# One ring of six tiles for keys and values, output weights in two loads, three modulation terms in one load

## The chip, the cores and the metric

The kernel runs on one core of one Trainium2 chip. The metric is the device time of one execution in microseconds (us). Before the change the median of three runs is 386.42 us (386.37 to 386.49). The profile is one execution, taken by the hardware profiler.

## The reference

One decode step of a block for 4 sequences with one token each, in float32. Six modulation terms come from the condition `c`; attention with 32 query heads over 8 key and value heads of 4096 cached tokens follows, and then a small token-mixing network.

```python
mod = (silu(c) @ w_mod).reshape(4, 6, 1, 512)        # sa, ca, ga, sb, cb, gb = terms 0 to 5
h = layernorm(x) * (1 + ca) + sa
q = h @ wq                                           # 32 heads of 128
scores = einsum("bhqd,bhkd->bhqk", q, k) * 128**-0.5 # k, v: (4, 8, 4096, 128), each used by 4 query heads
o = einsum("bhqk,bhkd->bhqd", softmax(scores), v)
x = x + ga * (o.reshape(4, 1, 4096) @ wo)
h = layernorm(x) * (1 + cb) + sb
u = gelu(einsum("bsd,sf->bdf", layernorm(h), w1) + b1)
x = x + gb * (einsum("bdf,fs->bds", u, w2) + b2).transpose(0, 2, 1)
```

Keys and values are 134 MB of the 157 MB that the core reads.

## The kernel before

The work is cut into 32 pairs, one for each sequence and key head (pair i is sequence i // 8, head i % 8). A pair needs K_i and V_i, each 128 partitions by 4096 floats, 16 KB a row. All loads are issued from SyncE's queue (SP), which works in order: a load that waits holds all that stand behind it. The sixteen DMA engines take the loads one after the other.

**Where data lies.** The pool `ring` has three slots of 32 KB a partition. A slot holds in turn the weights of terms 0 and 1 (`wm01`), half of `wq` (twice), K0 with K1 (`kk`), and then K_(i+2) with V_i (one load of 4096 KB from `kv[i]`, called kv0, kv1, ... below, issued by `load_pair`). A slot is used again when all that read it are done. Terms 2 to 4 (`wm24`) take a slot for a while, in two loads. The output weights `wo` lie outside the ring in four tiles of two heads each, called wo0, wo2, wo4 and wo6, each with a load of 2048 KB and rows of 16 KB (`load_wo`).

**The loop.** After a prologue (terms 0 and 1, the queries, the scores of pairs 0 and 1) a loop over i = 0 to 23 issues `load_pair(i + 1)`, computes the scores of pair i + 2 and their maximum, turns the exponentials of pair i + 1, projects pair i - 1 with `wo`, multiplies the weights of pair i with V_i in two halves (`values`, name `pv`), and has the exponentials of pair i + 2 taken by ScalarE in between. At the end of the pass i = 2 the terms 2 to 4 are computed (`mod`): for each a set of wide matmuls that read `wm24` (name `pm2` to `pm4`), a copy by ScalarE, a set of narrow matmuls (`pc2` to `pc4`) and another copy. After the loop the last eight pairs follow in an order written out by hand (`PLAN`), with the loads among the steps: `LP` a pair, `LK` keys, `LV` values, `LW` term 5.

The order of the loads is thus: terms 0 and 1, small inputs, wq, kk, kv0, wo0, kv1, kv2, wo2, terms 2 and 3, term 4, kv3, kv4, wo4, kv5, kv6, wo6, kv7 to kv27, K30, K31, V28 to V31, term 5.

Of the kernel before, what the change touches and what calls it, by code (L numbers as in the profile page):

```python
# [8 lines left out]
F32 = mybir.dt.float32  # L9
# [18 lines left out]
@with_exitstack  # L28
def adaln_decode(ctx: ExitStack, tc: tile.TileContext, small, x, wmod, wq, kk, kv, vv, wo, out):
    nc = tc.nc  # L30
    pad = ctx.enter_context(tc.tile_pool(name="pad", bufs=1))
    ring = ctx.enter_context(tc.tile_pool(name="ring", bufs=3))
    wos = ctx.enter_context(tc.tile_pool(name="wos", bufs=1))
# [13 lines left out]
    xr = wk.tile([P, D], F32, name="xr", tag="yw", bufs=1)[0:B]  # L47
    wm01 = ring.tile([P, 2, 4, D], F32, name="wm01", tag="kv")
    nc.sync.dma_start(wm01, wmod[0])
    nc.sync.dma_start(sm, small)  # L50
    nc.sync.dma_start(xr, x)
    wqt = []
    for k in range(0, 4, 2):
        t = ring.tile([P, 2, HQ * DH], F32, name=f"wq{k}", tag="kv")
        nc.sync.dma_start(t, wq[k // 2])
        wqt += [t[:, 0], t[:, 1]]
    w1, b1, w2 = sm[:, 0:NF], sm[:, NF:2 * NF], sm[:, 2 * NF:3 * NF]
# [98 lines left out]

    KT, VT, WM = {}, {}, {}

    def slots():
        return ring.tile([P, 2, SK], F32, name="kv", tag="kv")  # L160

    def key(t, i):
        KT[i] = t

    def value(t, i):
        VT[i] = t.rearrange("p (j d) -> p j d", d=DH)

    def load_first():
        t = slots()
        nc.sync.dma_start(t, kk)  # L170
        key(t[:, 0], 0)
        key(t[:, 1], 1)

    def load_pair(i):
        t = slots()
        nc.sync.dma_start(t, kv[i])
        key(t[:, 0], i + 2)
        value(t[:, 1], i)

    def load_wo(h):  # L180
        nc.sync.dma_start(wo_p[h // 2], wo[h // 2])

    def load_wm24():
        w = ring.tile([P, 3, 4, D], F32, name="wm24", tag="kv")
        nc.sync.dma_start(w[:, 0:2], wmod[1])
        nc.sync.dma_start(w[:, 2], wmod[2][:, 0])
        for e in range(3):
            WM[2 + e] = w[:, e]

    def load_wm5():  # L190
        t = slots().rearrange("p s (k n) -> p (s k) n", n=D)
        nc.sync.dma_start(t[:, 0:4], wmod[2][:, 1])
        WM[5] = t[:, 0:4]
        return t[:, 4:6]

    def load_key(t, i):
        nc.sync.dma_start(t, kv[i - 2][:, 0])
        key(t, i)

    def load_v(t, i, cuts):  # L200
        value(t, i)
        src = (kv[i][:, 1] if i < NS - 2 else vv[i - NS + 2]).rearrange("p (j d) -> p j d", d=DH)
        for lo, hi in zip(cuts, cuts[1:]):
            nc.sync.dma_start(VT[i][:, lo:hi], src[:, lo:hi])

# [20 lines left out]
    def scores(i):  # L226
        b, h = divmod(i, HKV)
        S[i] = s = ps_s.tile([P, 1024], F32, name=f"s{i}", tag="s")
        for n in range(2):
            for c in range(4):  # L230
                mm(s[32 * c:32 * c + 32, n * 512:(n + 1) * 512], QT[:, b, h, :],  # L231
                   KT[i][:, (n * 4 + c) * 512:(n * 4 + c + 1) * 512], start=True, stop=True)

    def row_max(i):
# [50 lines left out]
    def values(i, ks):  # L285
        if ks[0] == 0:
            PV[i] = ps_v.tile([P, 4 * DH], F32, name="pv", tag="pv")
        pT = PL[i][0]
        for k in ks:
            q = k % 4  # L290
            mm(PV[i][32 * q:32 * q + 32, :], pT[:, 128 * k:128 * k + 128:4],  # L291
               VT[i][:, 4 * k:4 * k + 4, :].rearrange("p j d -> p (j d)"), start=(k < 4), stop=(k >= 4))

    def values_narrow(i, ks, pv=None):
        if ks[0] == 0:
            PV[i] = ps_v.tile([P, DH], F32, name="pvn", tag="pv") if pv is None else pv
        pv = PV[i]
        pT = PL[i][0].rearrange("p (k r) -> p k r", r=32)
        top = 32 if i < NS - 1 else 30
        for k in ks:  # L300
            for j in range(4 * k, min(4 * k + 4, top)):
                c = j % 4
                mm(pv[32 * c:32 * c + 32, :], pT[:, j, :], VT[i][:, j, :], start=(k == 0), stop=(j + 4 >= top))  # L303

    def values_turned(i):
# [31 lines left out]
    def project(i, pa=None, between=None):  # L337
        b, h = divmod(i, HKV)
        oT = OT[i]
        if pa is None:  # L340
            pa = ps_m.tile([P, D], F32, name="pa", tag="m")
            for g in range(REP):
                mm(pa[32 * g:32 * g + 32, :], oT[:, g:g + 1].to_broadcast([P, 32]), wo_t[h][:, g, :],  # L343
                   start=True, stop=True)
        else:
            for g in range(REP):
                for c in range(4):
                    mm(pa[32 * c:32 * c + 32, :], oT[:, g:g + 1].to_broadcast([P, 32]),  # L348
                       wo_t[h][:, g, c * P:(c + 1) * P], start=(g == 0 and h == HKV - 2),
                       stop=(g == REP - 1 and h == HKV - 1))  # L350
                if between and g == 1:
                    between()
# [199 lines left out]
    def finish(b, pg, py, hb, wr):  # L552
        uu = ring.tile([P, 16, D], F32, name="uu", tag="kv")
        for js in ((0,), (1,), (2, 3, 4), (5, 6, 7), (8, 9, 10), (11, 12), (13,)):
# [34 lines left out]
    def fold_gate(gate, es):  # L589
        for e in es:  # L590
            w = wo_t[HKV - 2 + e // REP][:, e % REP]
            dv.tensor_tensor_reduce(w, w, gate, 1.0, 0.0, OP.mult, OP.add, rowsum[:, e:e + 1])
# [15 lines left out]

    load_first()
    load_pair(0)  # L610
    load_wo(0)
    for i in range(2):
# [5 lines left out]
    for i in range(NS - HKV):  # L618
        load_pair(i + 1)
        if i in (1, 3, 5):  # L620
            load_wo(i + 1)
        if i == 1:
            load_wm24()
        scores(i + 2)
# [22 lines left out]
        if mix:  # L647
            mix.outer(i % HKV)
        if i == 2:
            for t in range(2, 5):  # L650
# [4 lines left out]
                else:  # L655
                    nc.scalar.activation(dst, pm, AF.Copy)
        if i == NS - HKV - 2:
            gate = spread_gate()
# [3 lines left out]
    mix, row = Mixer(B - 2), Mixer(B - 1)  # L662
    pve = pgx = pc = ep = spare = slot = None
    gates = list(range(2 * REP))
    cuts = {NS - 1: (0, 16, 24, 28, 30, 32), NS - 2: (0, 16, 32)}
    last, halves = [(0, 1, 2, 3), (4, 5), (6,), (7,)], [(0, 1), (2, 3), (4, 5), (6, 7)]
    PLAN = """
    a23 v24.0 A23 p23 t25.0 P23 F R v24.1 LP25 G s26 t25.1 M H V24 LP26 Q a24 S26 v25.0 N s27 x A24 f p24 g
    x LP27 m26 S27 P24 m27 X26 X27 b26 B26 e26 x b27 v25.1 c g t26.1 l25 t26.0 B27 s28 V25 c g L25
    v26.0 v26.1 S28 x l26 f a25 L26 V26 A25 x m28 p25 LT X28 e27 c a26 P25 t27.0 A26 b28 s29 f B28 p26 e28  # L670
    LK30 t27.1 S29 P26 v27.0 m29 l27 g LK31 T t28.1 X29 LT t28.0 s30 L27 S30 b29 v27.1 B29 e29 l28 m30 V27
    LV28 L28 a27 g X30 t29.1 t29.0 l29 L29 s31 A27 LV29 b30 p27 x B30 S31 c c m31 e30 P27 X31 v28.0 f LT LV30
    b31 v28.1 B31 f e31 LV31 l30 V28 L30 t30.1 l31 L31 a28 t31.1 A28 p28 v29.0 v29.1 t30.0 f P28 V29 v30.0 a29
    v30.1 A29 LW p29 f v30.2 v30.3 t31.0 P29 g V30 Y y a30 A30 p30 E x v31.0 f v31.1 v31.2 v31.3 V31 z31 a31 I A31 j p31
    g T2 zs za zx zq c c zm zb0 T3 zv zb1 zw0 zn zc
    """
# [7 lines left out]
    for step in PLAN.split():  # L684
# [17 lines left out]
        elif op == "p":  # L702
            project(i, pgx[:, 4] if i >= NS - 2 else None, mean_last if i == NS - 1 else None)
        elif op == "LT":
            slot = slots()
        elif op == "LK":
            load_key(slot[:, i % 2], i)
        elif op == "LV":
            load_v(slot[:, i % 2], i, cuts.get(i, (0, 32)))
        elif op == "LW":  # L710
            spare = load_wm5()
        elif op == "x":
            mix.expand(spare if mix.n == 6 else None)
        elif op == "f":
# [74 lines left out]
```

## Time and profile before

| | |
|---|---|
| median of three runs | 386.42 us |
| span of the profiled execution, first to last instruction | 384.7 us |
| TensorE matmul busy | 298.7 us (78%) |
| VectorE busy | 198.2 us (52%) |
| ScalarE busy | 112.2 us (29%) |
| read from HBM | 157.32 MB |
| mean granted TensorE clock | 0.883 |

The profiled execution's span leaves out what lies around the first and the last instruction; no time of its own besides the span is given, so it is read against the runs, which are 1.7 us longer. Rows of a timeline have the start, the length, the engine, the line of the kernel, the operation, what is written and read, a count, and in brackets the idle time before and what ended it. L231 is the scores, L291 the values, L215 and L221 the wide and narrow matmuls of the terms 2 to 4. SPq is SyncE's queue, L176 a pair's load, L181 a load of `wo`, L170 the load `kk`, L49 that of terms 0 and 1. Rows of waits have the waiting engine and line, the one waited for, the total in us, the times and the longest. Rows of stretches give for each engine its busy time, then the granted clock of TensorE (PEclk), the busy share of the DMA engines and GB/s.

### The profile page before, as it was taken

What the parts mean: (1) busy time and instruction counts of PE and PEld (TensorE: products, weight loads), DVE (VectorE), ACT (ScalarE), POOL (GpSimd) and SP (SyncE); (2) the same over time, 40 slices, a digit from 0 to 9 for tenths busy, and PEclk for the clock granted to TensorE, in tenths of its full rate; (3) what the DMA queues carried; (4) which work ended last, traced back from release to release, by engine and by line L of the source; (5) the groups of instructions that cost most, each with busy time, mean ns of one, the idle gap of its engine ahead of it and who ended that gap; (6) DMA issues with size and microseconds to landing.
All of it is one profiled execution on the core that took longest, in us unless ns stands there. A gap on an engine that the chain in (4) does not pass through costs nothing.

```text
span 384.7 us, 5604 instructions
## 1 busy us (share of the span) xinstructions
PE 298.7 (78%) x2380; PEld 117.2 (30%) x2380; DVE 198.2 (52%) x407; ACT 112.2 (29%) x144; POOL 7.7 (2%) x33
## 2 busy tenths in 40 slices
PE   0856777866966949979877878788888887999984
PEld 0112122311323313334322222342222343333653
DVE  1130251620451424664866545557665567778757
ACT  1001111121110110212567311124575105657276
POOL 1100000000000000000000000000000000000000
PEclk9989555985695685998999998999999999999999
DMA  8999999999999999999999999999999999999930
GB/s 331 433 433 436 411 453 433 409 432 436 423 441 433 434 436 436 434 436 431 429 425 433 428 433 434 429 433 431 429 434 436 434 436 432 424 417 423 418 122 3
DMA packets 7409, 157.69 MB, mean 410 GB/s; under 512 B 964, under 2 KB 1236, under 8 KB 1496
## 3 DMA queue, kind: packets, MB, share of 16 engines
q1 hardware_dynamic: 7376, 157.33, 95.4%
q8 instruction: 18, 0.29, 0.3%
q14 instruction: 7, 0.06, 0.0%
q10 hardware_dynamic: 8, 0.00, 0.0%
HBM read 157.32 MB, written 0.01 MB: 409 GB/s over the span
## 4 chain that ended last, share of the span: by engine, by line
DMA 60%; PE 29%; DVE 7%; ACT 2%; issue 1%; POOL 0%; SPq 0%; POOLq 0%; DVEq 0%
DMA kv<-in_kv 58%; PE s L231 8%; PE pv L291 7%; PE s L122 2%; PE qs L138 2%; DVE m L236 2%; DVE p L267 2%; DMA sm<-in_small 2%; PE pa L343 2%; PE pt L328 2%; ACT uu L562 1%; PE pb L251 1%; PE pve L303 1%; PE pm L240 1%; PE pgx L348 1%
## 5 line engine op out<-in xcount | busy, mean ns | idle before, releaser
L231 PE MATMUL s<-kv,QT 128*32 128x512 f32 x512 | 75.2, 714 | 38.9 <-DMA kv<-in_kv 37.0
L236 DVE TENSOR_REDUCE m<-s 128x1 f32<-128x1024 f32 x32 | 39.2, 1224 | 96.0 <-PE s L231 95.9
L261 ACT ACTIVATE p<-s,nm 128x1024 f32<-128x1024 f32 x32 | 35.7, 1115 | 180.6 <-DVE nm L256 180.5
L291 PE MATMUL pv<-kv,p 128*32 128x512 f32 x464 | 69.8, 670 | 0.7 <-DMA kv<-in_kv 0.7
L231 PEld LDWEIGHTS s<-kv,QT 128*32 128x32 f32 x512 | 15.8, 123 | 84.0 <-DMA kv<-in_kv 52.5
L328 PEld LDWEIGHTS pt<-g,po 128*128 128x128 f32 x236 | 31.1, 205 | 27.2 <-issue 19.9
L343 PE MATMUL pa<-wo,oT 128*32 128x512 f32 x240 | 34.6, 648 | 4.6 <-DVE oT L335 4.4
L328 PE MATMUL pt<-g,po 128*128 128x4 f32 (+2 forms) x236 | 33.9, 267 | 1.5 <-DVE po L314 1.0
L267 DVE STREAM_TRANSPOSE p<-p 128x1024 f32<-128x1024 f32 x25 | 30.9, 1234 | 0.0
L314 DVE COPY po<-pv 128x512 f32<-128x512 f32 x29 | 20.0, 688 | 16.8 <-PE pv L291 16.7
L245 DVE TENSOR_REDUCE mx<-pm 1x128 f32<-1x512 f32 x32 | 21.3, 669 | 1.1 <-PE pm L240 1.1
L442 DVE TENSOR_SCALAR u<-hb,wr,sm 128x512 f32<-128x512 f32 x40 | 19.9, 541 | 1.9 <-POOL wr L437 1.0
L506 ACT ACTIVATE u<-u 128x1024 f32<-128x1024 f32 x20 | 20.4, 1051 | 1.5 <-DVE u L442 1.4
L361 DVE TENSOR_TENSOR acc<-acc,pa 128x512 f32<-128x512 f32 x26 | 17.8, 686 | 4.3 <-PE pa L343 4.2
L261 ACT ACT_TABLE_LOAD x11 | 14.1, 1283 | 20.3 <-DVE nm L256 20.2
L251 PEld LDWEIGHTS pb<-neg,mx 1*128 1x128 f32 x64 | 10.4, 202 | 28.2 <-DVE mx L245 26.5
L122 PE MATMUL s<-wm,sT 128*4 128x512 f32 x16 | 9.1, 732 | 10.6 <-DVE sT L108 10.6
L506 ACT ACT_TABLE_LOAD x13 | 16.7, 1283 | 0.2
L291 PEld LDWEIGHTS pv<-kv,p 128*32 128x32 f32 x464 | 13.4, 146 | 7.2 <-issue 3.1
L240 PE MATMUL pm<-ident,m 128*1 128x128 f32 x32 | 9.3, 289 | 7.4 <-DVE m L236 3.5
L251 PE MATMUL pb<-neg,mx 1*128 1x1 f32 x64 | 13.1, 271 | 2.1 <-DVE mx L245 2.1
L453 PE MATMUL py<-u,sm 128*32 128x512 f32 x80 | 14.4, 616 | 0.0
(158 smaller groups left out, 214.7 us busy)
## 6 DMA issues: line engine op xcount, KB each, us to landing
kv<-in_kv SPq DMA_DIRECT2D x28, 4096.0 KB, 21.9
wq<-in_wq SPq DMA_DIRECT2D x2, 4096.0 KB, 16.3
wo<-in_wo SPq DMA_DIRECT2D x4, 2048.0 KB
kv<-in_kv SPq DMA_DIRECT2D x4, 2048.0 KB, 20.3
wm<-in_wmod SPq DMA_DIRECT2D x2, 2048.0 KB, 14.8
kv<-in_kk SPq DMA_DIRECT2D x1, 4096.0 KB
kv<-in_vv SPq DMA_DIRECT2D x3, 1024.0 KB
wm<-in_wmod SPq DMA_DIRECT2D x1, 1024.0 KB
```

What stands on the lines that cost most here:

```text
L231: mm(s[32 * c:32 * c + 32, n * 512:(n + 1) * 512], QT[:, b, h, :], KT[i][:, (n * 4 + c) * 512:(n * 4 + c + 1) * 512], start=True, stop=True)
L236: dv.tensor_reduce(M[i], S[i], axis=AX.X, op=OP.max)
L245: dv.tensor_reduce(mx, M[i].rearrange("o (c r) -> o r c", c=4).unsqueeze(1).to_broadcast([1, 4, 32, 4]), axis=AX.X, op=OP.max)
L251: mm(pb, M[i].rearrange("o c r -> o (c r)"), neg1, start=True, stop=True)
L261: nc.scalar.activation(p, S[i], AF.Exp, bias=M.pop(i), accum_out=l)
L267: dv.transpose(PL[i][0], PL[i][0])
L291: mm(PV[i][32 * q:32 * q + 32, :], pT[:, 128 * k:128 * k + 128:4], VT[i][:, 4 * k:4 * k + 4, :].rearrange("p j d -> p (j d)"), start=(k < ...
L314: dv.tensor_copy(PV[i], pv)
L328: mm(pt, po[:, c * DH:(c + 1) * DH], sel.unsqueeze(1).to_broadcast([P, m, REP]), start=(c == 0), stop=(c == n - 1))
L343: mm(pa[32 * g:32 * g + 32, :], oT[:, g:g + 1].to_broadcast([P, 32]), wo_t[h][:, g, :], start=True, stop=True)
L442: dv.tensor_scalar(u[:, e, :], hb, wr[:, j:j + 1], b1[:, j:j + 1], op0=OP.mult, op1=OP.add)
L506: nc.scalar.activation(u, u, AF.Gelu_apprx_tanh)
```

## The change

The three slots become one tile `RING` of six parts of 16 KB a partition, of which a pair's load takes two neighbours. The four tiles of `wo` become one, `wo_t`, loaded in two loads of 4096 KB with rows of 32 KB (heads 0 to 3, heads 4 to 7: wo0-3 and wo4-7 below). Terms 0 and 1 are loaded into the place of heads 0 and 1 of `wo_t`, terms 2 to 4 with one load of 3072 KB and rows of 24 KB into the place of heads 4 to 6. A list `LOADS` has all later loads in order; `advance(name)` is called when the code that reads a part has been written, and issues from the head of the list what may go: a pair when what its two parts held has been read, wo0-3 after terms 0 and 1, wo4-7 after terms 2 to 4 (`"M2"`). The terms 2 to 4 are computed at the end of the pass i = 1 instead of i = 2. The steps for loads are gone from `PLAN`.

```diff
-    wm01 = ring.tile([P, 2, 4, D], F32, name="wm01", tag="kv")
-    nc.sync.dma_start(wm01, wmod[0])
+    RING = ring.tile([P, 6, SK], F32, name="kv")
+    wo_t = wos.tile([P, HKV, REP, D], F32, name="wo")
+    wm01, wm24 = wo_t[:, 0:2], wo_t[:, 4:7]
+    nc.sync.dma_start(wm01, wm0)
...
-    wo_p = [wos.tile([P, 2, REP, D], F32, name=f"wo{h}") for h in range(0, HKV, 2)]
-    wo_t = [wo_p[h // 2][:, h % 2] for h in range(HKV)]
...
+    held, read = [("Q", 0), ("Q", 0), ("Q", 1), ("Q", 1), None, None], {None, ("Q", 0), ("Q", 1)}
...
+    def queue():
+        q = [entry(["K0", "K1"], kk)]
+        for i in range(NS - 4):
+            q.append(entry([f"K{i + 2}", f"V{i}"], kv[i]))
+        for i in (NS - 2, NS - 1):
+            q.append(entry([f"K{i}"], kv[i - 2][:, 0]))
+        for i in range(NS - 4, NS):
+            q.append(entry([f"V{i}"], kv[i][:, 1] if i < NS - 2 else vv[i - NS + 2]))
+        q.append(entry(["W5"], wm5))
+        q.insert(2, ("wo", "M0", wo_t[:, 0:4], wo[0]))
+        q.insert(4, ("wo", None, wm24, wm2))
+        q.insert(6, ("wo", "M2", wo_t[:, 4:8], wo[1]))
+        return q
+
+    LOADS, at = queue(), [4]
+
+    def advance(name=None):
+        read.add(name)
+        while LOADS:
+            kind, names, *rest = LOADS[0]
+            if kind == "wo":
+                if names not in read:
+                    return
+                nc.sync.dma_start(*rest)
+            else:
+                n, p = len(names), at[0]
+                if any(h not in read for h in held[p:p + n]):
+                    return
...
+                held[p:p + n] = names
+                at[0] = (p + n) % 6
...
+            LOADS.pop(0)
...
-        load_pair(i + 1)
-        if i in (1, 3, 5):
-            load_wo(i + 1)
-        if i == 1:
-            load_wm24()
...
-        if i == 2:
+        if i == 1:
             for t in range(2, 5):
                 pm = mod(t)
...
+            advance("M2")
```

What it does to SyncE's queue, from the load of wq on. `DMAHW` stands for a counter of landed loads (there are eight, taken in turn), `PE` for a wait on TensorE. Before, the terms 2 to 4 (`wm_337`) come after kv2 and wo2, and their slot is asked for by kv5, the row after wo4 (`wo_130`):

```order
L176 DMA kv<-in_kv 128x8192 [waits DMAHW3_49,PE_49]
L181 DMA wo_128<-in_wo 128x4096
L176 DMA kv<-in_kv 128x8192 [waits DMAHW4_49,PE_49]
L176 DMA kv<-in_kv 128x8192 [waits DMAHW5_49,DMAHW1_49,PE_49]
L181 DMA wo_129<-in_wo 128x4096 [waits DMAHW2_49]
L185 DMA wm_337<-in_wmod 128x4096 [waits DMAHW6_49,PE_49]
L186 DMA wm_337<-in_wmod 128x2048
L176 DMA kv<-in_kv 128x8192 [waits DMAHW0_49,PE_49]
L176 DMA kv<-in_kv 128x8192 [waits DMAHW1_49,PE_49]
L181 DMA wo_130<-in_wo 128x4096 [waits DMAHW7_49]
L176 DMA kv<-in_kv 128x8192 [waits DMAHW4_49,DMAHW3_49,PE_49]
```

After, from kk on: the terms (`in_wm`, 128x6144) stand between kv1 and kv2, and the load after kv2 is wo4-7:

```order
L204 DMA kv<-in_kk 128x8192
L204 DMA kv<-in_kv 128x8192 [waits DMAHW3_49,PE_49]
L186 DMA wo<-in_wo 128x8192 [waits DMAHW0_49]
L204 DMA kv<-in_kv 128x8192 [waits DMAHW4_49,PE_49]
L186 DMA wo<-in_wm 128x6144 [waits DMAHW1_49]
L204 DMA kv<-in_kv 128x8192 [waits DMAHW5_49,DMAHW2_49,PE_49]
L186 DMA wo<-in_wo 128x8192 [waits DMAHW1_49,PE_49]
L204 DMA kv<-in_kv 128x8192 [waits DMAHW6_49]
L204 DMA kv<-in_kv 128x8192 [waits DMAHW0_49]
L204 DMA kv<-in_kv 128x8192 [waits DMAHW2_49,PE_49]
```

So the load that waits for the reading of the terms has moved from three loads behind them to one load behind them, and kv3 and kv4, which ask for no later reading, have moved behind it.

On TensorE, the end of the pass i = 2 before (the values of pair 2, the three terms, the scores of pair 5, `s5`):

```order
L291 MATMUL pv_427<-kv_334,p_325 32x512 x4
L251 MATMUL pb_432<-neg1_87,mx_425 128x1
L291 MATMUL pv_427<-kv_334,p_325 32x512 x4
L215 MATMUL pm2_445<-wm24_337,sT8_134 32x512 x4
L221 MATMUL pc2_452<-ym_450,g32_122 32x128 x4
L215 MATMUL pm3_458<-wm24_337,sT8_134 32x512 x4
L221 MATMUL pc3_465<-ym_463,g32_122 32x128 x4
L215 MATMUL pm4_471<-wm24_337,sT8_134 32x512 x4
L221 MATMUL pc4_478<-ym_476,g32_122 32x128 x4
L231 MATMUL s5_487<-kv_392,QT_124 32x512 x8
```

And the end of the pass i = 1 after it (the values of pair 1, the terms read from `wo`, the scores of pair 4, `s4`):

```order
L300 MATMUL pv_362<-kv_90,p_282 32x512 x4
L260 MATMUL pb_367<-neg1_87,mx_360 128x1
L300 MATMUL pv_362<-kv_90,p_282 32x512 x4
L223 MATMUL pm2_380<-wo_91,sT8_129 32x512 x4
L229 MATMUL pc2_387<-ym_385,g32_121 32x128 x4
L223 MATMUL pm3_393<-wo_91,sT8_129 32x512 x4
L229 MATMUL pc3_400<-ym_398,g32_121 32x128 x4
L223 MATMUL pm4_406<-wo_91,sT8_129 32x512 x4
L229 MATMUL pc4_413<-ym_411,g32_121 32x128 x4
L239 MATMUL s4_422<-kv_90,QT_123 32x512 x8
```

The three terms have moved ahead of the scores of pair 4, one pass earlier; the rest of TensorE's order is the same.

More of the change, by code (lines that the diff above doesn't have):

```diff
@@ L28, in adaln_decode @@
 @with_exitstack
-def adaln_decode(ctx: ExitStack, tc: tile.TileContext, small, x, wmod, wq, kk, kv, vv, wo, out):
+def adaln_decode(ctx: ExitStack, tc: tile.TileContext, small, x, wm0, wm2, wm5, wq, kk, kv, vv, wo, out):
     nc = tc.nc
     pad = ctx.enter_context(tc.tile_pool(name="pad", bufs=1))
-    ring = ctx.enter_context(tc.tile_pool(name="ring", bufs=3))
+    ring = ctx.enter_context(tc.tile_pool(name="ring", bufs=1))
     wos = ctx.enter_context(tc.tile_pool(name="wos", bufs=1))
@@ L53, in adaln_decode @@
     for k in range(0, 4, 2):
-        t = ring.tile([P, 2, HQ * DH], F32, name=f"wq{k}", tag="kv")
-        nc.sync.dma_start(t, wq[k // 2])
-        wqt += [t[:, 0], t[:, 1]]
+        nc.sync.dma_start(RING[:, k:k + 2], wq[k // 2])
+        wqt += [RING[:, k], RING[:, k + 1]]
     w1, b1, w2 = sm[:, 0:NF], sm[:, NF:2 * NF], sm[:, 2 * NF:3 * NF]
@@ L155, in adaln_decode @@
     nc.scalar.activation(prep[:, 0], px, AF.Copy)
[L157 to L204, printed above, removed]
+    KT, VT, WM = {}, {}, {2 + e: wm24[:, e] for e in range(3)}
+    held, read = [("Q", 0), ("Q", 0), ("Q", 1), ("Q", 1), None, None], {None, ("Q", 0), ("Q", 1)}
@@ new lines, in adaln_decode, with entry @@
+    cuts = {NS - 1: (0, 16, 24, 28, 30, 32), NS - 2: (0, 16, 32)}
+    def entry(names, src):
+        return ("ring", names, src)
+    def queue():
[11 more added lines that the diff above has]
+        return q
@@ new lines, in adaln_decode @@
+    LOADS, at = queue(), [4]
[11 more added lines that the diff above has]
+                    return
+                for k, nm in enumerate(names):
+                    t, i = RING[:, p + k], int(nm[1:])
+                    if nm[0] == "K":
+                        KT[i] = t
+                    elif nm[0] == "V":
+                        VT[i] = t.rearrange("p (j d) -> p j d", d=DH)
+                    else:
+                        WM[i] = t.rearrange("p (k n) -> p k n", n=D)[:, 0:4]
+                held[p:p + n] = names
+                at[0] = (p + n) % 6
+                if names[0] == "W5":
+                    nc.sync.dma_start(WM[5], rest[0])
+                elif len(names) > 1:
+                    nc.sync.dma_start(RING[:, p:p + n], rest[0])
+                elif names[0][0] == "K":
+                    nc.sync.dma_start(RING[:, p], rest[0])
+                else:
+                    cs = cuts.get(i, (0, 32))
+                    v = rest[0].rearrange("p (j d) -> p j d", d=DH)
+                    for lo, hi in zip(cs, cs[1:]):
+                        nc.sync.dma_start(VT[i][:, lo:hi], v[:, lo:hi])
+            LOADS.pop(0)
@@ L232, in scores @@
                    KT[i][:, (n * 4 + c) * 512:(n * 4 + c + 1) * 512], start=True, stop=True)
+        advance(f"K{i}")
     def row_max(i):
@@ L292, in values @@
                VT[i][:, 4 * k:4 * k + 4, :].rearrange("p j d -> p (j d)"), start=(k < 4), stop=(k >= 4))
+        if ks[-1] == 7:
+            advance(f"V{i}")
     def values_narrow(i, ks, pv=None):
@@ L303, in values_narrow @@
                 mm(pv[32 * c:32 * c + 32, :], pT[:, j, :], VT[i][:, j, :], start=(k == 0), stop=(j + 4 >= top))
+        if ks[-1] == 7:
+            advance(f"V{i}")
     def values_turned(i):
@@ L342, in project @@
             for g in range(REP):
-                mm(pa[32 * g:32 * g + 32, :], oT[:, g:g + 1].to_broadcast([P, 32]), wo_t[h][:, g, :],
+                mm(pa[32 * g:32 * g + 32, :], oT[:, g:g + 1].to_broadcast([P, 32]), wo_t[:, h, g, :],
                    start=True, stop=True)
@@ L348, in project @@
                     mm(pa[32 * c:32 * c + 32, :], oT[:, g:g + 1].to_broadcast([P, 32]),
-                       wo_t[h][:, g, c * P:(c + 1) * P], start=(g == 0 and h == HKV - 2),
+                       wo_t[:, h, g, c * P:(c + 1) * P], start=(g == 0 and h == HKV - 2),
                        stop=(g == REP - 1 and h == HKV - 1))
@@ L552, in finish @@
     def finish(b, pg, py, hb, wr):
-        uu = ring.tile([P, 16, D], F32, name="uu", tag="kv")
+        uu = RING[:, 4:6].rearrange("p s (k n) -> p (s k) n", n=D)
         for js in ((0,), (1,), (2, 3, 4), (5, 6, 7), (8, 9, 10), (11, 12), (13,)):
@@ L590, in fold_gate @@
         for e in es:
-            w = wo_t[HKV - 2 + e // REP][:, e % REP]
+            w = wo_t[:, HKV - 2 + e // REP, e % REP]
             dv.tensor_tensor_reduce(w, w, gate, 1.0, 0.0, OP.mult, OP.add, rowsum[:, e:e + 1])
@@ L607, in mean_last @@
         dv.tensor_copy(mu, pm)
-    load_first()
-    load_pair(0)
-    load_wo(0)
+    advance("M0")
     for i in range(2):
@@ L662, in adaln_decode @@
     mix, row = Mixer(B - 2), Mixer(B - 1)
-    pve = pgx = pc = ep = spare = slot = None
+    pve = pgx = pc = ep = None
     gates = list(range(2 * REP))
-    cuts = {NS - 1: (0, 16, 24, 28, 30, 32), NS - 2: (0, 16, 32)}
     last, halves = [(0, 1, 2, 3), (4, 5), (6,), (7,)], [(0, 1), (2, 3), (4, 5), (6, 7)]
     PLAN = """
[L668 to L674, printed above, removed]
+    a23 v24.0 A23 p23 t25.0 P23 F R v24.1 G s26 t25.1 M H V24 Q a24 S26 v25.0 N s27 x A24 f p24 g
+    x m26 S27 P24 m27 X26 X27 b26 B26 e26 x b27 v25.1 c g t26.1 l25 t26.0 B27 s28 V25 c g L25
+    v26.0 v26.1 S28 x l26 f a25 L26 V26 A25 x m28 p25 X28 e27 c a26 P25 t27.0 A26 b28 s29 f B28 p26 e28
+    t27.1 S29 P26 v27.0 m29 l27 g T t28.1 X29 t28.0 s30 L27 S30 b29 v27.1 B29 e29 l28 m30 V27
+    L28 a27 g X30 t29.1 t29.0 l29 L29 s31 A27 b30 p27 x B30 S31 c c m31 e30 P27 X31 v28.0 f
+    b31 v28.1 B31 f e31 l30 V28 L30 t30.1 l31 L31 a28 t31.1 A28 p28 v29.0 v29.1 t30.0 f P28 V29 v30.0 a29
+    v30.1 A29 p29 f v30.2 v30.3 t31.0 P29 g V30 Y y a30 A30 p30 E x v31.0 f v31.1 v31.2 v31.3 V31 z31 a31 I A31 j p31
     g T2 zs za zx zq c c zm zb0 T3 zv zb1 zw0 zn zc
@@ L703, in adaln_decode @@
             project(i, pgx[:, 4] if i >= NS - 2 else None, mean_last if i == NS - 1 else None)
[L704 to L711, printed above, removed]
         elif op == "x":
-            mix.expand(spare if mix.n == 6 else None)
+            mix.expand(RING[:, 2].rearrange("p (k n) -> p k n", n=D)[:, 4:6] if mix.n == 6 else None)
         elif op == "f":
@@ L770 @@
     v = a["A_v_cache"].reshape(NS, P, SK * DH // P)
+    wm = a["w_mod"].reshape(4, P, 6, D).transpose(1, 2, 0, 3)
     arrays = {
@@ L773 @@
         "x": con(a["A_x"].reshape(B, D)),
-        "wmod": con(a["w_mod"].reshape(4, P, 3, 2, D).transpose(2, 1, 3, 0, 4)),
+        "wm0": con(wm[:, 0:2]),
+        "wm2": con(wm[:, 2:5]),
+        "wm5": con(wm[:, 5]),
         "wq": con(a["A_wq"].reshape(2, 2, P, HQ * DH).transpose(0, 2, 1, 3)),
@@ L778 @@
         "vv": con(v[NS - 2:]),
-        "wo": con(a["A_wo"].reshape(HKV // 2, 2, REP, DH, D).transpose(0, 3, 1, 2, 4)),
+        "wo": con(a["A_wo"].reshape(2, 4, REP, DH, D).transpose(0, 3, 1, 2, 4)),
     }
```

3 lines of the change are left out of this document (1 added, 2 removed).

## The prediction

> **What bounds the kernel now.** I read the page's slices first, then the chain, then the stretches of time, and last the load queue beside TensorE around the place of the change.
>
> ```profile
> span 384.7 us, 5604 instructions
> ...
> DMA  8999999999999999999999999999999999999930
> GB/s 331 433 433 436 411 453 433 409 432 436 423 441 433 434 436 436 434 436 431 429 425 433 428 433 434 429 433 431 429 434 436 434 436 432 424 417 423 418 122 3
> DMA packets 7409, 157.69 MB, mean 410 GB/s; under 512 B 964, under 2 KB 1236, under 8 KB 1496
> ...
> DMA 60%; PE 29%; DVE 7%; ACT 2%; issue 1%; POOL 0%; SPq 0%; POOLq 0%; DVEq 0%
> ```
> ```profile
> core 0: us, PE busy (x) PEld busy (x) DVE busy (x) ACT busy (x) POOL busy (x), PEclk, DMA share, GB/s
> 2.00:3.00 1.00, 0.00 (x0) 0.00 (x0) 0.94 (x2) 0.00 (x1) 0.00 (x0) 1.00 0.39 82
> 3.00:83.00 80.00, 53.34 (x291) 15.79 (x291) 23.34 (x47) 7.93 (x17) 2.31 (x15) 0.81 1.00 431
> 3.00:366.00 363.00, 286.33 (x2116) 108.93 (x2120) 184.67 (x370) 98.13 (x126) 6.27 (x24) 0.88 1.00 431
> ```
> The DMA engines are busy from 3 us to 366 us without a pause (share 1.00 at 431 GB/s), and TensorE keeps up. So the kernel is one stream of 157 MB and what is left to compute when its last keys come. The reader should take two things from this: a change that moves no fewer bytes can gain only in the rate, and any time in which the queue runs empty is paid in full, since nothing later can catch up. The end hangs on the stream as well:
>
> ```profile
> 343.17 1.92 PE L231 MATMUL s<-kv,QT 128*32 128x512 f32 x16 [0.60 <-DMA kv<-in_kv]
> ```
> TensorE waits there for the keys of a late pair, and from there on the chain is compute in an order that the change leaves alone. The work after it comes later by what the keys come later.
>
> **The change, part by part.** The runs are at 386.42 us and this execution spans 384.7, so 1.7 us lie around the span. I sum against 384.7 and add 1.7.
>
> *Kept in place, in a new order.* The bytes are the same, but what stands in the queue at the start is not. Before, the queue has wo0 (2048 KB), kv1, kv2, wo2, the two loads of terms 2 to 4, kv3. After, it has wo0-3 (4096 KB), kv1, terms 2 to 4 (3072 KB), kv2, wo4-7, kv3. The load of wo4-7 writes over the three terms, so it has to wait until TensorE has read the last of them, and SyncE issues in order, so kv3 and all that follows wait behind it. In the trace the wait on the terms costs nothing, because a lot is in flight. The sizes (count, KB each) from the page's load issues, the wait as SyncE's queue had it, and SyncE's issues in time:
>
> ```profile
> kv<-in_kv SPq DMA_DIRECT2D x28, 4096.0 KB, 21.9
> wq<-in_wq SPq DMA_DIRECT2D x2, 4096.0 KB, 16.3
> wo<-in_wo SPq DMA_DIRECT2D x4, 2048.0 KB
> ...
> wm<-in_wmod SPq DMA_DIRECT2D x2, 2048.0 KB, 14.8
> kv<-in_kk SPq DMA_DIRECT2D x1, 4096.0 KB
> ...
> wm<-in_wmod SPq DMA_DIRECT2D x1, 1024.0 KB
> ```
> ```profile
> SPq L176 <- PE pm L215: 6.5, 1, 6.5
> ```
> ```profile
> 0.72 0.39 SPq L49 DMA_DIRECT2D wm<-in_wmod  x1
> ...
> 19.72 0.33 SPq L170 DMA_DIRECT2D kv<-in_kk  x1
> ...
> 71.80 8.61 SPq L176 DMA_DIRECT2D kv<-in_kv  x2
> 80.45 0.42 SPq L181 DMA_DIRECT2D wo<-in_wo  x1
> 91.49 14.30 SPq L176 DMA_DIRECT2D kv<-in_kv  x2
> ```
> Row 71.80 holds kv3 and kv4. kv5 waits for the terms and is issued at 91.49, when they are read. Issued by then are kv3, kv4 and wo4 on top of all before, 45.1 MB; at 431 GB/s and 34.6 MB by 83 us that lasts to about 107 us, so 16 us of cover. After the change the load that waits stands right behind kv2. [...]
>
> *When the queue runs empty.* Up to the end of kv2 the new order has 2048 + 38 KB (terms 0, 1 and the small inputs), 8192 (wq), five loads of 4096 (kk, kv0, wo0-3, kv1, kv2) and 3072 KB: 34.64 MB. The rows above give 0.08 + 80 x 0.431 = 34.56 MB by 83.0 us. So it ends at 83.2 us.
>
> *When the terms are read.* TensorE in the stretch that matters:
>
> ```profile
> 59.52 1.08 PE L291 MATMUL pv<-kv,p 128*32 128x512 f32 x4
> 63.14 3.30 PE L231 MATMUL s<-kv,QT 128*32 128x512 f32 x16 [2.54 <-DMA kv<-in_kv]
> ...
> 70.64 1.09 PE L291 MATMUL pv<-kv,p 128*32 128x512 f32 x8
> ```
> ```profile
> 82.51 1.47 PE L215 MATMUL pm<-wm,sT 128*32 128x512 f32 x8 [2.49 <-DMA wm<-in_wmod]
> 84.67 0.66 PE L221 MATMUL pc<-ym,g 128*32 128x128 f32 x8 [0.70 <-ACT ym L218]
> 85.73 1.94 PE L215 MATMUL pm<-wm,sT 128*32 128x512 f32 x8 [0.40 <-ACT prep L656]
> 88.44 0.66 PE L221 MATMUL pc<-ym,g 128*32 128x128 f32 x8 [0.78 <-ACT ym L218]
> 89.49 1.94 PE L215 MATMUL pm<-wm,sT 128*32 128x512 f32 x8 [0.40 <-ACT prep L656]
> ```
> ```profile
> 94.58 3.64 PE L231 MATMUL s<-kv,QT 128*32 128x512 f32 x16 [1.72 <-DMA kv<-in_kv]
> ```
> ```profile
> 63.10:71.80 8.70, 8.22 (x53) 2.74 (x53) 3.92 (x7) 0.80 (x1) 0.00 (x0) 0.83 0.97 420
> 94.50:105.40 10.90, 10.82 (x57) 4.07 (x61) 4.04 (x7) 0.79 (x1) 0.00 (x0) 0.59 0.97 418
> 118.80:131.00 12.20, 12.14 (x57) 4.33 (x61) 4.04 (x7) 1.21 (x2) 0.00 (x0) 0.51 0.98 422
> 143.20:155.20 12.00, 11.95 (x57) 4.33 (x61) 4.04 (x7) 1.21 (x2) 0.00 (x0) 0.52 1.01 437
> 82.50:91.50 9.00, 6.65 (x40) 0.97 (x40) 0.00 (x0) 1.75 (x4) 0.00 (x0) 0.53 1.06 455
> ```
> The last fence is a table of stretches, with the columns named above. (1) kv1 is in at 63.1 before. With 2048 KB more ahead of it, 2.10 MB / 0.431 = 4.9 us, scores of pair 3 start at 68.0. (2) Then the rest of that pass of the loop runs, to the second half of values(1). The row of 63.10 shows 8.6 us for it, at a mean clock of 0.83; three other passes that start after TensorE had stood still took 10.9, 12.2 and 12.0 us, at clocks near one half. After the change TensorE stands still before it from 60.6 to 68.0, longer than before, so it starts cold like those. I take the mean of the four, 10.9. The terms' load is in by then: it follows kv1 by 3.15 MB / 0.431 = 7.3 us, so at 75.3 us. (3) The three terms: before, 8.9 us from the first matmul to the last reading (82.51 to 91.43), nearly all at half clock (0.53). At full clock the two kinds of matmul take about half of 1.94 and 0.66 us, and the waits for ScalarE (0.78 and 0.40) stay: 2 x (0.97 + 0.78 + 0.33 + 0.40) + 0.97 = 5.9 us, an estimate. After a cold pass the clock has just come back, but three short terms with pauses hardly hold it; I take 7.2, in the middle. Together: 68.0 + 10.9 + 7.2 = 86.1 us. At the ends: 68.0 + 8.6 + 5.9 = 82.5, and 68.0 + 12.2 + 8.9 = 89.1.
>
> *The restart.* wo4-7 starts into an empty queue. The nearest row is the start of the program: the first load is issued at 0.72 us, and the stream has its full rate from 3.0 with 82 GB/s in the microsecond before, so the stream runs as if it had begun somewhat after 2; some engines move data before that. I bound it by 1.0 and 1.9 us and take 1.5. [...] No row shows a restart in mid-kernel.
>
> So the stream stands still from 83.2 to 86.1 + 1.5 = 87.6: 4.4 us. At the ends: 82.5 + 1.0 - 83.2 = 0.3, and 89.1 + 1.9 - 83.2 = 7.8 us. Nothing hides it: wo4-7, kv3 and kv4 then go out together (29 us of stream), and kv5 asks only for values(2), which ends some 12 us after the terms, so the queue fills again.
>
> *Longer rows and fewer loads.* wo goes from four loads of 16 KB rows to two of 32 KB, terms 2 to 4 from 16 and 8 KB rows to 24 KB: 11.5 MB.
>
> ```profile
> 4.00:7.00 3.00, 0.00 (x0) 0.00 (x0) 0.00 (x0) 0.00 (x0) 0.00 (x0) 1.00 1.02 437
> 10.00:26.00 16.00, 11.20 (x28) 2.39 (x32) 4.93 (x17) 0.00 (x0) 1.28 (x5) 0.97 1.01 436
> 355.00:361.00 6.00, 5.54 (x106) 4.10 (x102) 4.36 (x11) 3.02 (x4) 0.00 (x0) 1.00 1.00 425
> ```
> The three rows move 16 KB rows, 32 KB rows and mostly 8 KB rows. Between 437 and 436 there is no gain; between 425 and 436, 11.5 MB take 0.7 us less. I take 0.2, nearer to the row with 16 KB, which most of it had.
>
> *The ring of six.* Keys are let go after the scores, values after their own matmuls, each for itself; pairs still ask for both. Before 63 us and in the last 60 us the queue is never empty (share 1.00), so earlier issues only lengthen the queue: 0. kk no longer waits for the first terms: it was issued at 19.72, when terms 0 and 1 and wq, 10.5 MB, still had the queue until about 27 us; 0. Were that cover gone, each such load would start up to 1.9 us late, as the restart. The three terms move ahead of one pass on TensorE, ScalarE and VectorE: the scores of pair 4 start after them, some 3 us after kv2 is in, and the exponentials of pair 4 behind ScalarE's copies; the wait for pair 5, whose keys come at about 108 us, covers both, else it would be those 3 us. Address changes on TensorE and the `uu` tile that lies in two ring tiles: 0, the same instructions on the same engines.
>
> Sum: 384.7 + 4.4 - 0.2 = 388.9, and 1.7 around it: 390.6 us.
>
> **Rivals.** (B) *The clock comes back early.* If full clock is granted within the first scores, as at 63.10 (8.6 us), the terms are read at about 68.0 + 8.6 + 6.6 = 83.2 and the stop is 1.5 us: 384.7 + 1.5 - 0.2 + 1.7 = 387.7. For it: that very pass did so before. Against: three of the four rows with a cold start did not. [...]
>
> (C) *The stop is hidden.* If the terms are read before 81.7 (83.2 less the restart), nothing is left of it: 386.2. It needs less than the lowest sum of (2) and (3), 14.5, by nearly a microsecond.
>
> (D) *Faster.* Fewer, longer loads raise the rate: 0.7 us as above at most, and for each of the three loads saved the difference between 436 GB/s here and 431 in the long run, 4.19 MB / 0.431 - 4.19 MB / 0.436 = 0.1 us, 0.3 in all: 385.4. It decides only if the stop is under 1 us, that is if the terms are read by about 82.7. For it: the earliest sum, 82.5. [...]
>
> (E) *More than the one stop.* TensorE stays at half clock and needs 12 us for a pass while a pair's data needs 9.7, so kv6 to kv9 are issued late and the queue runs out again; some 3 us more: 394. Against it: the row at 94.50 recovers within its pass.
>
> **Chances.** A (forecast) 0.58, B 0.24, C 0.07, D 0.04, E 0.07. A's own range is 388.7 to 393; with most of B below and the bound of 7.8 us above (394.0, rarely reached) the range is 387.2 to 393.6. A measurement of this kernel can tell about 0.2%, 0.8 us. Faster by that is D, 0.04; within it are C and the lowest edge of B, 0.08; slower the rest, 0.88.
>
> **What would show it.** The GB/s of the slice around 83 to 88 us should fall (by up to half of a 9.6 us slice), and the DMA share be 1.00 before and after. The issue of wo4-7 should wait for TensorE's last reading of the terms, at 84 to 89 us, with kv3 and kv4 right behind it. Scores of pair 3 should start near 68, those of pair 5, which stand behind wo4-7 and kv3, near 108 instead of 94.6, and from the pass after wo6 of before on everything should lie about 4 us later. The keys awaited at 343.1 should come near 347. I am wrong if the queue never runs empty, if TensorE reads the terms before 82, or if the late keys come at the same time in spite of a stop.

## The result and the profile after

The change makes the kernel slower by 0.7%: 388.51 us median of 11 executions against 386.49, a ratio of 1.0072 (95% interval 1.005 to 1.0093). The 11 times lie in two groups: seven from 387.78 to 388.57 us, at a mean granted clock of 0.898 to 0.915, and four from 391.47 to 391.91 us, at 0.873 to 0.886. The profiled execution took 388.26 us and spans 386.5, 1.8 us more than the one before. By its time it belongs to the lower group, so its trace should show the smaller stop of the two.

The page of the changed kernel, the slices of 9.66 us:

```profile
span 386.5 us, 5592 instructions
...
PEclk9989666799589699899999998969999989899999
DMA  8999999989999999999999999999999999999920
GB/s 330 434 434 434 432 434 418 450 348 432 434 432 434 429 427 434 432 434 432 434 433 431 430 434 432 434 434 432 434 432 434 432 434 430 421 424 422 416 106 4
```

One slice falls out of the row, the ninth (77 to 87 us) with 348 GB/s. Before, no slice between the first and the tail is under 409. SyncE's queue and TensorE there, in the changed kernel:

```profile
47.20 0.33 SPq L204 DMA_DIRECT2D kv<-in_kv  x1
82.81 0.33 SPq L186 DMA_DIRECT2D wo<-in_wo  x1
83.19 236.24 SPq L204 DMA_DIRECT2D kv<-in_kv  x25
```
```profile
67.60 3.64 PE L239 MATMUL s<-kv,QT 128*32 128x512 f32 x16 [9.14 <-DMA kv<-in_kv]
71.17 1.33 PE L341 MATMUL pt<-g,po 128*128 128x4 f32 x8
...
76.43 1.04 PE L223 MATMUL pm<-wo,sT 128*32 128x512 f32 x8
78.19 0.43 PE L229 MATMUL pc<-ym,g 128*32 128x128 f32 x8 [0.72 <-ACT ym L226]
79.02 1.06 PE L223 MATMUL pm<-wo,sT 128*32 128x512 f32 x8 [0.40 <-ACT prep L662]
80.86 0.43 PE L229 MATMUL pc<-ym,g 128*32 128x128 f32 x8 [0.78 <-ACT ym L226]
81.68 1.06 PE L223 MATMUL pm<-wo,sT 128*32 128x512 f32 x8 [0.40 <-ACT prep L662]
...
105.27 3.64 PE L239 MATMUL s<-kv,QT 128*32 128x512 f32 x16 [13.43 <-DMA kv<-in_kv]
```

From 47.2 us on SyncE issues nothing until TensorE has read the last term (81.68 + 1.06 = 82.74): wo4-7 goes out at 82.81, kv3 behind it. The first scores are at half clock (3.64 us), and the next matmuls are already quicker (1.33 us where a cold pass before had 1.87): the granted clock is 0.50 up to 71.5 us and 1.00 from 72 to 95. The stretches around it (columns: busy time of PE, PEld, DVE, ACT, POOL, then PEclk, DMA share, GB/s):

```profile
75.00:82.00 7.00, 4.71 (x50) 1.39 (x50) 1.01 (x3) 2.96 (x6) 0.00 (x0) 1.00 1.04 447
82.00:84.50 2.50, 1.17 (x16) 0.16 (x8) 0.29 (x1) 0.60 (x1) 0.00 (x0) 1.00 0.80 236
90.00:366.00 276.00, 222.07 (x1755) 89.12 (x1747) 160.60 (x319) 89.06 (x106) 3.96 (x9) 0.93 1.00 431
```

The queue ran empty between 82 and 84.5 us, and never again. (A packet of data counts in the stretch in which it starts, so that a share can be a little over 1.) The delay shows far behind. The scores of pair 17, which wait for their keys, before and after:

```profile
220.80 1.93 PE L231 MATMUL s<-kv,QT 128*32 128x512 f32 x16 [0.51 <-DMA kv<-in_kv]
```
```profile
222.29 1.92 PE L239 MATMUL s<-kv,QT 128*32 128x512 f32 x16 [0.36 <-DMA kv<-in_kv]
```

They come 1.5 us later. The theory is thus: the whole cost is the time in which the stream stops, and it is set by the moment at which TensorE has read the terms; two groups of times are there because the clock of TensorE sets that moment. The rivals: the cost lies in the layout (ring of six, one tile of output weights, rows); or part of a stop is taken up by slack later; or the groups have another cause than the clock.

### The profile page after: what moved, and what is told of

Same layout as the page of the kernel before. It is cut to its first block, busy times and chain, and to the rows that moved or that the text cites. A ratio compares the mean times of both kernels' runs of the same rounds, so it can differ in the third digit from the quotient of the medians.

```text
span 386.5 us, 5592 instructions
## 1 busy us (share of the span) xinstructions
PE 289.3 (75%) x2380; PEld 114.1 (30%) x2380; DVE 198.0 (51%) x407; ACT 112.2 (29%) x144; POOL 7.7 (2%) x33
## 4 chain that ended last, share of the span: by engine, by line
DMA 55%; PE 31%; DVE 10%; ACT 2%; issue 1%; SPq 1%; POOL 0%; POOLq 0%
DMA kv<-in_kv 46%; DMA kv<-in_kk 9%; PE s L239 9%; PE pv L300 8%; DVE m L245 3%; PE pa L356 3%; DVE p L276 3%; PE pt L341 2%; PE pb L260 1%; PE py L466 1%; ACT kv L575 1%; PE pve L314 1%; PE pm L249 1%; DVE po L327 1%; PE pl L284 1%
## 5 line engine op out<-in xcount | busy, mean ns | idle before, releaser
L239 PE MATMUL s<-kv,QT 128*32 128x512 f32 x512 | 72.5, 690 | 53.2 <-DMA kv<-in_kv 50.8
L300 PE MATMUL pv<-kv,p 128*32 128x512 f32 x464 | 68.2, 656 | 0.0
L239 PEld LDWEIGHTS s<-kv,QT 128*32 128x32 f32 x512 | 14.6, 117 | 95.6 <-DMA kv<-in_kv 68.8
L260 PEld LDWEIGHTS pb<-neg,mx 1*128 1x128 f32 x64 | 9.6, 187 | 27.1 <-DVE mx L254 25.4
L121 PE MATMUL s<-wo,sT 128*4 128x512 f32 x16 | 8.7, 702 | 10.4 <-DVE sT L107 10.4
L260 PE MATMUL pb<-neg,mx 1*128 1x1 f32 x64 | 12.3, 259 | 2.1 <-DVE mx L254 2.1
```

Source lines behind the costliest of these rows:

```text
L260: mm(pb, M[i].rearrange("o c r -> o (c r)"), neg1, start=True, stop=True)
```

## The experiments

**A pair between.** The list is changed by one place, so that kv3 goes ahead of the load that waits.

```diff
-        q.insert(6, ("wo", "M2", wo_t[:, 4:8], wo[1]))
+        q.insert(7, ("wo", "M2", wo_t[:, 4:8], wo[1]))
```

> The changed kernel with one entry of the list moved: kv3 goes ahead of wo4-7, so the load that waits for the terms has 4.19 MB (9.7 us) more in flight. If the whole cost is the stop of the queue, the stop is gone at either clock (terms read by 89 us at the latest, the stream lasts to 93), all executions lie together and the time is 386.2 to 386.6, the kernel before within 0.2%; the share of the DMA engines is 1.00 from 80 to 95 us. If the cost lies in the ring of six, the one tile of output weights or the row lengths, it stays at 388 and 391.5 us.

Measured: 386.55 us (386.49 to 386.61 in 11 executions), ratio to the kernel before 0.9998 (0.9989 to 1.0007). Its issues and its keys of pair 17:

```profile
47.42 11.01 SPq L204 DMA_DIRECT2D kv<-in_kv  x2
83.05 0.33 SPq L186 DMA_DIRECT2D wo<-in_wo  x1
```
```profile
220.72 1.92 PE L239 MATMUL s<-kv,QT 128*32 128x512 f32 x16 [0.43 <-DMA kv<-in_kv]
```

wo4-7 waits as long as in the changed kernel, to 83.05, but kv3 is in flight meanwhile. The cost is gone, and with it the two groups, though the mean clock still varies from 0.887 to 0.925. So the layout, the ring of six and the longer rows together cost nothing and gain nothing that the runs can tell: all of the loss hangs on that one place in the list.

**The terms a pass earlier.** The other way out: wo4-7 stays behind kv2, but the terms are loaded ahead of kv1 and computed at the end of the pass i = 0.

```diff
-        q.insert(4, ("wo", None, wm24, wm2))
+        q.insert(3, ("wo", None, wm24, wm2))
...
-        if i == 1:
+        if i == 0:
             for t in range(2, 5):
```

> The changed kernel with the load of the terms 2 to 4 one place earlier, ahead of kv1, and the terms computed at the end of the pass i = 0, where TensorE waits for kv1 anyway. wo4-7 still stands right behind kv2 and still waits for the terms. The terms land at about 66 us and are read by 72 at full and 75 at half clock, some 8 us before the queue would run empty at 83. If only the moment at which the waiting load is released counts, the stop is gone in all executions: 386.3 to 386.7, as where a pair was put between. If a load that waits right behind kv2 costs something in itself, or if kv1 coming 7 us later does (its pass then ends later), the time is 387.5 or more.

Measured: 386.56 us (386.40 to 386.66 in 12 executions), ratio 0.9997 (0.9988 to 1.0006).

```profile
65.35 1.94 PE L223 MATMUL pm<-wo,sT 128*32 128x512 f32 x8 [8.42 <-DMA wo<-in_wm]
...
72.82 1.94 PE L223 MATMUL pm<-wo,sT 128*32 128x512 f32 x8 [0.40 <-ACT prep L662]
...
75.96 3.64 PE L239 MATMUL s<-kv,QT 128*32 128x512 f32 x16
```
```profile
74.81 0.33 SPq L186 DMA_DIRECT2D wo<-in_wo  x1
```

The terms run at half clock throughout (1.94 us), and it does not matter: they are read at 74.8 us, 8 us before the queue would be empty. A load that waits right behind kv2 costs nothing in itself, and TensorE does most of the terms in a time in which it waited for keys.

**The terms a pass later.** The opposite test, a longer wait: the terms computed at the end of the pass i = 2, as before the change, with the new order of loads.

```diff
-        if i == 1:
+        if i == 2:
             for t in range(2, 5):
```

> The changed kernel with the terms 2 to 4 computed at the end of the pass i = 2, as in the kernel before, the loads in the changed order. wo4-7 then waits for the scores of pair 4 (84.6 us, kv2), that pass (8 to 12 us) and the terms (6 to 9): read at 99 to 106 us, issue to data 1.1. If an empty queue is paid in full, the stop is 17 to 24 us and the time 403 to 410 us. If later slack takes up part of a stop, it is less, for instance half of it: 395 to 398.

Measured: 408.28 us (405.90 to 409.75 in 4 executions), ratio 1.0558 (1.0528 to 1.0588). The profiled execution took 407.41 us.

```profile
101.75 0.33 SPq L186 DMA_DIRECT2D wo<-in_wo  x1
```
```profile
80.00:104.00 24.00, 15.10 (x105) 4.85 (x101) 5.72 (x10) 3.55 (x7) 0.00 (x0) 0.78 0.18 66
```
```profile
241.35 1.92 PE L239 MATMUL s<-kv,QT 128*32 128x512 f32 x16 [0.35 <-DMA kv<-in_kv]
```

The queue is empty for most of 80 to 104 us, and pair 17 comes 20.6 us later than without a stop. Nothing of it is taken up later.

**A part that need not wait.** Head 7 of the output weights lies where no term is. It goes first, without a wait, and heads 4 to 6 wait.

```diff
-        q.insert(6, ("wo", "M2", wo_t[:, 4:8], wo[1]))
+        q.insert(6, ("wo", None, wo_t[:, 7], wo[1][:, 3]))
+        q.insert(7, ("wo", "M2", wo_t[:, 4:7], wo[1][:, 0:3]))
```

> The changed kernel with the load of heads 4 to 7 cut in two: head 7, whose place holds no term, goes first and without a wait (1.05 MB, 2.4 us of stream), heads 4 to 6 wait for the terms. If the cost is the time in which the queue is empty, it falls by 2.4 us: the lower group from 388.1 to about 386.4 (its stop of 1.5 us is gone), the upper one from 391.5 to about 389.1. If it is the mere presence of a load that waits, or anything in the layout, both groups stay.

Measured: 388.41 us (387.41 to 389.70 in 6 executions), ratio 1.0048 (1.0031 to 1.0065). The times do not fall into two groups as expected, and none reached 386.4; against the 388.51 of the changed kernel they show no gain. The trace is clearer than the times: in the profiled execution (388.38 us) the waiting load was issued at 84.88, 2.1 us later than in the trace of the changed kernel, and pair 17 began at the same time.

```profile
84.88 0.33 SPq L187 DMA_DIRECT2D wo<-in_wo  x1
```
```profile
222.22 1.92 PE L240 MATMUL s<-kv,QT 128*32 128x512 f32 x16 [0.35 <-DMA kv<-in_kv]
```

By the table further below, that issue without head 7 would have put pair 17 at about 224.4. So head 7's 1.05 MB, 2.4 us of stream, has taken off 2.2 us, nearly what it is long, in this one trace.

**Two more traces of the changed kernel**, meant to catch the upper group.

> The changed kernel once more, for a trace of the other group of times. At 388 us: full clock from about 72 us, terms read at 82.7, as in the trace at hand. At 391.5 us: half clock through the pass i = 1, from 67.6 to about 80, and into the terms, read at about 86, and the queue empty for 3 us longer. If instead the terms are read at the same time in both groups, something else parts them.

> The same as the look before it: two looks, since about one in three executions is of the upper group.

They took 389.29 and 390.34 us, so neither is of the upper group; there are times between the groups too. The later one (the third trace of the changed kernel) shows the clock at work:

```profile
71.50 1.87 PE L341 MATMUL pt<-g,po 128*128 128x4 f32 x8
...
73.73 1.94 PE L356 MATMUL pa<-wo,oT 128*32 128x512 f32 x8
...
83.73 1.06 PE L223 MATMUL pm<-wo,sT 128*32 128x512 f32 x8 [0.40 <-ACT prep L662]
```
```profile
84.85 0.33 SPq L186 DMA_DIRECT2D wo<-in_wo  x1
```
```profile
224.31 1.92 PE L239 MATMUL s<-kv,QT 128*32 128x512 f32 x16 [0.36 <-DMA kv<-in_kv]
```

Here the same matmuls of the pass i = 1 stay at half clock longer (1.87 and 1.94 us), the terms are read 2.0 us later (84.79), and pair 17 begins 2.0 us later. In the trace of the kernel with the terms a pass later, whose code is the same up to that point, the half clock lasts through the whole pass:

```profile
67.90:80.20 12.30, 12.17 (x53) 4.02 (x53) 4.04 (x7) 1.21 (x2) 0.00 (x0) 0.51 1.00 431
```

After such a pass, to 80.1 us, the terms at full clock (6.3 us, as in the trace after) would be read at 86.4. That fits the upper group by the table below, but no execution of that group has been traced, so for the group itself it is an estimate.

**Keeping TensorE warm**, by 20 and then by 36 added matmuls at the end of the pass i = 0.

```diff
         copy_v(i)
+        if i == 0:
+            pd = ps_e.tile([P, D], F32, name="pd", tag="e")
+            for w in range(20):                # then 36
+                c = w % 4
+                mm(pd[32 * c:32 * c + 32, :], g32, QT[:, 0:2].rearrange("p b h c -> p (b h c)"), start=True, stop=True)
```

> The changed kernel with 20 matmuls of 512 columns added at the end of the pass i = 0, where TensorE waits from about 60 to 67.6 us; their result is not used. If the two groups of times (388 and 391.5) come from the clock at which the pass i = 1 and the terms run, full clock is there when the scores of pair 3 start: the pass takes 7.2 us, the terms start when their load lands (75 us) and are read by about 81.4, the stop is under 0.5 us, and all executions lie at 386.3 to 387.0. If the two groups have another cause (memory, the end of the kernel), they stay 3.4 us apart. If the added matmuls run too long, the scores of pair 3 start after 67.6 and the time is above 388.

> As the kernel with 20 added matmuls at the end of the pass i = 0, but with 36, since 20 ended at 61.4 us and left TensorE idle for 6.5 us before the scores of pair 3, which then ran at half clock. 36 take 8 us at full clock and end at 65 to 68. If the clock at the scores of pair 3 sets the time, it is full there in most executions, the terms are read at 81.5 to 83 and the times lie at 386.5 to 388.5 with none above 390. If the clock is not the cause, the spread stays as it was (387.8 to 391.9). Where the added matmuls end after 67.6, they cost what they overrun, up to 2 us.

Measured: 388.92 us (388.40 to 390.69 in 6 executions) with 20, ratio 1.0064 (1.0046 to 1.0082), and 389.10 us (388.16 to 392.01 in 6) with 36, ratio 1.008 (1.0055 to 1.0105). As tests of the times both missed what was expected. The traces say why for the first: the 20 ended early, and the scores of pair 3 were cold again. (The profile lists each of these matmuls twice, so 20 are x40.)

```profile
56.91 4.47 PE L657 MATMUL pd<-QT,g 128*32 128x512 f32 x40
67.87 3.64 PE L239 MATMUL s<-kv,QT 128*32 128x512 f32 x16 [6.49 <-DMA kv<-in_kv]
```

With 36 the profiled execution (388.16 us) had what was meant:

```profile
57.55 7.90 PE L657 MATMUL pd<-QT,g 128*32 128x512 f32 x72
67.65 1.92 PE L239 MATMUL s<-kv,QT 128*32 128x512 f32 x16 [2.20 <-DMA kv<-in_kv]
```
```profile
81.28 0.33 SPq L186 DMA_DIRECT2D wo<-in_wo  x1
```

The pass is warm, the terms are read at 81.2, and pair 17 is only 0.5 us late (221.22). So the traces move with the clock as the theory says; that a warm pass removes the groups of times is not shown. And the span is 386.4 us, 1.6 more than with the pair between. At its end TensorE runs behind the stream and waits for no keys (none of the scores from 300.91 to 349.65 us has a wait ahead of it). A half clock there may have a part in it. This is the stretch from the scores of pair 25 to those of pair 26, first here, then in the kernel with the pair between:

```profile
300.90:316.40 15.50, 13.30 (x98) 5.24 (x97) 7.51 (x16) 1.80 (x3) 0.00 (x0) 0.89 0.99 428
```
```profile
299.90:313.80 13.90, 11.83 (x99) 5.09 (x97) 7.50 (x16) 1.80 (x3) 0.00 (x0) 1.00 1.00 431
```

It takes 1.6 us more at a mean clock of 0.89. But the kernel with the terms a pass earlier has a stretch as long there (299.87 to 315.67 us) and still spans 384.8, so this alone doesn't settle the 1.6 us; nor is it known what made the 392.01.

**Long rows alone.** The kernel before, with the output weights in two tiles and two loads.

```diff
-    wo_p = [wos.tile([P, 2, REP, D], F32, name=f"wo{h}") for h in range(0, HKV, 2)]
-    wo_t = [wo_p[h // 2][:, h % 2] for h in range(HKV)]
+    wo_p = [wos.tile([P, 4, REP, D], F32, name=f"wo{h}") for h in range(0, HKV, 4)]
+    wo_t = [wo_p[h // 4][:, h % 4] for h in range(HKV)]
...
-        if i in (1, 3, 5):
+        if i == 3:
             load_wo(i + 1)
```

> The kernel before with one part of the change alone: the output weights in two tiles of four heads with two loads of 4096 KB and rows of 32 KB, after kv0 and after kv4, where the queue is never empty. By the rate of long rows 0.0 to 0.7 us less than before, 0.1 to 0.2 expected: 386.3, not to be told from before. [...]

Measured: 386.45 us against 386.44, ratio 1.0004 (0.9995 to 1.0014). Neither the longer rows nor two loads fewer are worth anything that the runs can tell.

Put together, from the traces (the issue of the load that waits, the start of pair 17's scores, the execution's time, all in us):

| kernel | issue | pair 17 | time |
|---|---|---|---|
| pair between | 83.05, covered | 220.72 | 386.61 |
| terms a pass earlier | 74.81 | 220.66 | 386.64 |
| 36 added matmuls | 81.28 | 221.22 | 388.16 |
| changed | 82.81 | 222.29 | 388.26 |
| changed, second trace | 82.83 | 223.23 | 389.29 |
| changed, third trace | 84.85 | 224.31 | 390.34 |
| 20 added matmuls | 85.02 | 224.65 | 390.69 |
| terms a pass later | 101.75 | 241.35 | 407.41 |

From the third trace to the terms a pass later the issue moves by 16.90 us and pair 17 by 17.04: a stop is paid in full. Carried back to 220.7, the price begins at an issue of about 81.2 us. The bytes agree: from 82 to 200 us the DMA engines moved 431 GB/s with the pair between, 426 in the changed kernel, 418 in its third trace and 356 with the terms a pass later, which as time of the stream is 1.4, 3.6 and 20.5 us less. The second trace lies 0.9 us off the line, at an issue like that of the first. Its stream did not stop for longer, since it too moved 426 GB/s from 82 to 200 us; why its keys were complete later is open.

## Why the prediction was right

The mechanism, the place and the sign were right, and the time lay in the range. The size was about half of the forecast: 2.0 us (388.51 against 386.49) where 4.2 were expected (390.6 against 386.42). The range of 6.4 us takes in both groups of times, so that it was met says little about the size. By its steps:

- *The stream without slack:* shown by the terms a pass later, where 16.90 us more at the issue became 17.04 at pair 17.
- *The end of what is in flight, 83.2 us:* the share falls in 82 to 84.5. With the terms a pass later, where nothing follows for 18 us, no data starts after 83.4. Right.
- *Scores of pair 3 at 68.0:* 67.60.
- *When the terms are read, 86.1:* the term that was mis-sized. The pass took 8.8 us in the trace after (67.60 to 76.43), not 10.9, and the terms 6.3, not 7.2, so 82.74. It was not one value: 82.74, 82.78 and 84.79 were traced, and in the seven traces that have this pass from a cold start it took 8.5 to 12.2 us. Case B, "the clock comes back early" (387.7), is nearest to the median, and A (390.6) is nearer to the smaller group. The chances, 0.58 and 0.24, stood the wrong way round for these 11 executions; with seven against four, luck has a part in where the median fell. The error was to take the mean of passes whose times fall apart by the clock; and TensorE held full clock through the pauses of the terms (1.00 from 75 to 82 us), which was doubted.
- *The restart, 1.5 us:* counted from the stream's end at 83.2, a price that begins at an issue of 81.2 makes it 2.0. The trace with the terms a pass later, whose load is issued at 101.75, shows most of it:

```profile
101.75:102.60 0.85, 0.13 (x4) 0.13 (x8) 0.00 (x0) 0.60 (x1) 0.00 (x0) 1.00 0.00 0
102.00:103.00 1.00, 0.43 (x8) 0.16 (x8) 0.04 (x1) 0.41 (x1) 0.00 (x0) 1.00 1.45 393
```

No data starts until 102.6, about 1 us after the issue. Then a share of 1.45 goes with 393 GB/s, against 1.00 with 431 in the full stream, so the first packets take about 1.6 times as long as later ones (1.6 to 2.1 us for 32 KB in this trace, 1.7 to 2.0 behind the stop in the changed kernel's, against 1.2 in the full stream), which adds some 0.7 us.

- *Longer rows, -0.2:* 0.0 (386.45 against 386.44). *Ring of six and earlier issues, 0:* shown, together with the rows, by the pair between.
- *Rivals C and D:* C, terms read before 81.7, was not seen in the changed kernel. Its bound was half a microsecond too late: with 36 added matmuls they were read at 81.2, and pair 17 was still 0.5 us late. With the terms a pass earlier (74.8) no stop was left. D, faster by rows and fewer loads, fell with the long rows alone. E, a second stop, is not in the trace: 431 GB/s from 90 to 366 us.
- *The signs to look for:* wo4-7 was issued at 82.81, not at 84 to 89, and pair 5 began at 105.3, not 108, by the smaller stop. The scores that waited for their keys at 343.1 before come 1.8 us later, not 4, and the trace after shows no wait ahead of them:

```profile
344.94 1.92 PE L239 MATMUL s<-kv,QT 128*32 128x512 f32 x16
```

TensorE was behind the stream there, so the end did not hang on those keys as the prediction has it, though it came later by the same 1.8 us.

How early the clock comes back, the question of case B, differs from trace to trace: the same pass, started cold at 67.6 to 68.0, had full clock from about 71 or 72 us in three traces, 77 in three and 80 in one, that is after about 4, 9 and 12 us. In the longest TensorE was busy for 12.17 of 12.30 us, at a mean clock of 0.51. What brings the clock back is open.

## What to carry to other kernels

In a kernel bound by its stream of loads, ask of each load that waits how long the bytes issued ahead of it last. Here its wait had to end some 2 us before they did (81.2 against 83.2 us); what was missing was paid in full, however little the changed instructions cost. Order the list so that something which need not wait stands between the data and the load that overwrites it, or use the data earlier, in a time in which the engine waits anyway; both gave the whole loss back here (386.55 and 386.56 us). Neither beat the kernel before, whose stream was full already (431 GB/s from 3 to 366 us).

## What the hardware showed unexpectedly

The granted clock of one engine made the time of a kernel that is bound by its loads uncertain, by way of one wait: two traces of the same kernel differ by 2.0 us in the reading of the terms and in the keys of pair 17, and by 2.1 us in time (388.26 and 390.34). That the same makes the 3.3 us between the groups (388.2 against 391.5) is inferred, as said above. With cover in the queue the times of 11 executions lay within 0.12 us, while the mean clock varied nearly as much (0.887 to 0.925, against 0.873 to 0.915 in the changed kernel). That does not explain all of the spread: the kernel before and the one with long rows alone have cover too, and had a few executions at 387.6 to 388.1 us, for a reason that is not known. And a half clock of a few microseconds near the end, at 300 to 316 us, lengthened a stretch by 1.6 us (15.50 against 13.90, at a mean clock of 0.89 against 1.00), where TensorE had only about half a microsecond to spare (0.60 us of waiting at 343.17 before); one kernel with a stretch as long lost nothing by it, so what it costs is open.
